# Loading the query weights of a decode kernel in two halves of 64 partitions, from two DMA queues

## The chip, the cores and the metric

The kernel runs on one core of one Trainium2 chip. The metric is device time in microseconds (us) for one execution, from the median of several runs. The core has a matrix engine (TensorE, PE in the profile), a vector engine (VectorE, DVE), a scalar engine (ScalarE, ACT), GpSimd (POOL) and SyncE (SP), which in this kernel only issues transfers. Sixteen DMA engines move data between main memory and the on-chip memory of 128 partitions. SyncE and ScalarE each issue DMAs through a queue of their own; in the profile SPq and ACTq are these issues, q1 is SyncE's queue and q10 is ScalarE's.

## What is computed

One token of decoding through attention with cached keys and values, and beside it a gated feed-forward layer; a scalar gate mixes both. All data are float32.

```python
def reference(A_x, A_k_cache, A_v_cache, A_wq, A_wo, B_x, B_w1, B_w3, B_w2, gate_w):
    x = A_x                                          # (1, 1, 512)
    g = sigmoid((x * gate_w).sum(-1, keepdims=True))
    q = (x @ A_wq) as 32 heads of 128                # A_wq (512, 4096)
    k, v = caches (8 heads, 32768, 128), each head used by 4 query heads
    p = softmax(q k^T * 128 ** -0.5)
    a = (p v) as one row of 4096 @ A_wo              # A_wo (4096, 512)
    b = (silu(x @ B_w1) * (x @ B_w3)) @ B_w2         # 512 -> 1792 -> 512
    return g * a + (1 - g) * b
```

The two caches are 134.2 MB each, and everything else together is some 28 MB. wq is 8.39 MB.

## The kernel before

The code does not leave its order to a scheduler. `Program.add` (L44) takes each operation with the names of what it reads and writes, works out the semaphore waits from them, and appends it to its engine's list. Each engine then runs its list in the order in which it was written.

Loads are full tiles of 128 partitions x 64 KB, 8.39 MB. Two such buffers exist, `big[0]` (big_a in the profile) and `big[1]` (big_b). `load` (L190) issues a DMA on SyncE. SyncE's list holds the loads in the order in which the data are used: wq into big_a, the first key tile into big_b, the second key tile into big_a, the third into big_b, then the weights of the feed-forward layer, then key tiles (big_a) and value tiles (big_b) in turn, and at the end the last values, wo and w2. A load waits until the readers of its buffer are through; SyncE then waits with it, and what is behind it in the list waits too.

The start goes as follows:

- ScalarE issues the rows of the token (x) and of the gate (gate_w), 2 KB each, into one partition of `probs` (L201 and L202). Both count on the semaphore `row`.
- SyncE issues wq into big_a (L203, through L194), keys "A0" and "A1", then the first key tile.
- GpSimd and VectorE build constants (L213 to L238).
- TensorE turns the token's row into columns by four small transposes (`columns`, L251), which wait for both rows; VectorE copies them into `xp` (L259).
- TensorE multiplies xp with wq, which has its 512 rows as 128 partitions x 4 chunks (`part`, L263, matmuls at L268). They wait for wq and for xp.
- One more product and an activation make the gate (L279, L280).
- ScalarE copies the products out (L286), VectorE transposes them into the two `kt` buffers (L289), and ScalarE copies them from there into `win` (L296), 16 small copies; `winc` (L324) is the part that TensorE uses as weights for scores.

Then 16 key tiles follow. VectorE transposes a tile in eight parts into the two `kt` buffers (L346; one of them shows as aside in the profile), ScalarE copies three quarters of its second half aside (L318), TensorE multiplies (L330), and the scores are copied out (L358). From the fifth tile on, value tiles are multiplied in the same loop (L432). The second key tile goes to the buffer in which wq was, so that its load waits for the matmuls at L268. The third waits until the first is worked off.

The semaphores of SyncE's loads are nine, used in turn (`load1` and so on); wq has `load1`.

Of the kernel before, what the change touches and what calls it, by code (L numbers as in the profile page):

```python
# [13 lines left out]
P = 128  # L14
# [102 lines left out]
def kernel(  # L117
# [13 lines left out]
    nc = tc.nc  # L131
# [5 lines left out]
    NC = D // P  # L137
# [17 lines left out]
    pr = Program(nc, tc.alloc_semaphore)  # L155
    pe, dve, act, pool = (
        lambda fn, _e=e, **kw: pr.add(_e, fn, **kw) for e in ("PE", "DVE", "ACT", "POOL")
    )
    V, A, T = nc.vector, nc.scalar, nc.tensor

    def sbuf(name, *shape):
        return nc.alloc_sbuf_tensor(name, [P, *shape], F32)[:]

    big = [sbuf("big_a", 2 * R), sbuf("big_b", 2 * R)]
# [25 lines left out]
    def load(dst, src, writes, over=()):  # L190
        lanes[0] += 1
        lane = f"load{lanes[0] % 9}"
        return pr.add(
            "SP", lambda: nc.sync.dma_start(dst, src), writes=writes, over=[*over, lane], inc=lane, by=16, also=lane,  # L194
        )

    def region(b, z):
        return big[b][:, z * R:(z + 1) * R]


    for i, t in enumerate((x.rearrange("a b n -> (a b) n"), gate_w.rearrange("(o n) -> o n", o=1))):  # L201
        pr.add("ACT", lambda i=i, t=t: nc.scalar.dma_start(rows[i][0:1, :], t), writes=[f"row{i}"], inc="row", by=16)  # L202
    load(big[0], wq.rearrange("(p c) n -> p (c n)", c=NC), ["A0", "A1"])  # L203


    ident, ones, fold = sbuf("ident", P), sbuf("ones", P), sbuf("fold", 32)
# [1 line left out]
    spot, mask, xp = sbuf("spot", 16, 8), sbuf("mask", 16), sbuf("xp", NC, 32)  # L208
# [16 lines left out]
    for src, dst, view, axes in (  # L225
# [11 lines left out]
            reads=[src], writes=[dst])  # L237
# [24 lines left out]
    for c in range(NC):  # L262
        def part(c=c):  # L263
            t = region(0, c // 2)
            for b in range(2):
                for j in range(4):
                    o = ((c % 2) * HKV + 4 * b + j) * REP * DH
                    ins = T.matmul(  # L268
                        pf[b][32 * j:32 * j + 32, :], xp[:, c, :], t[:, o:o + REP * DH],
                        start=(c == 0), stop=(c == NC - 1),  # L270
                    )
            return ins
        pe(part, reads=["A0", "A1", "xp"], writes=["f0", "f1"])


    gpr, gsm = tmp[0:1, 1].rearrange("p b d -> p (b d)"), sbuf("gsm", 1)
# [5 lines left out]
        reads=["gate0"], writes=["gate1"])  # L282
# [414 lines left out]
    a, b, c, d = flips  # L697
# [67 lines left out]
```

## Time and profile before

| | before |
|---|---|
| median of 3 runs | 694.1 us (693.98 to 695.0) |
| the profiled execution's own time | 693.89 us |
| its span, first to last instruction | 692.1 us |
| busy: PE, DVE, ACT | 388.3, 370.1, 134.7 us |
| bytes moved | 296.35 MB |
| transfers issued by SyncE, by ScalarE | 296.23 MB, 0.01 MB |

The profile shows one execution. A row of the timeline has the start, the time taken, the engine, the line of the program, the operation with its output and input, and in brackets how long the engine was idle before it and what ended that. A row of the windows has the stretch, the busy time of each engine in it, the granted clock of TensorE, the share of the 16 DMA engines that was busy, and the rate in GB/s. A short window counts a request where it begins, so that the share of one window can lie above 1 and that of the next at 0.

### The profile page before, as it was taken

How to read it: one execution, taken by the hardware profiler on the slowest of the kernel's cores; microseconds unless marked ns; L12 is line 12 of the kernel's file. 1: busy time of each engine (PE TensorE's matmuls, PEld its weight loads, DVE VectorE, ACT ScalarE, POOL GpSimd, SP SyncE). 2: the span in 40 equal slices, each digit the busy share in tenths (PEclk: the TensorE clock that was granted, in tenths of full speed). 3: DMA queues.
4: the chain of work that ended last, by engine and by line, in shares of the span. 5: the costliest groups of instructions: out<-in, count | busy, mean ns of one | idle time of the engine just before them, and what ended most of it. 6: DMA issues, size and time to landing. Idle time of an engine off the chain costs nothing. (4 is left out here: it accounts for less than half of the span.)

```text
span 692.1 us, 5789 instructions
## 1 busy us (share of the span) xinstructions
PE 388.3 (56%) x2448; PEld 95.3 (14%) x2448; DVE 370.1 (53%) x259; ACT 134.7 (19%) x113; POOL 2.8 (0%) x15
## 2 busy tenths in 40 slices
PE   1537677566473636565564646364563646564457
PEld 0101111201010101201010101101010101211112
DVE  1049998493725637493826537492816547600701
ACT  0143323222303131220303131220303031100000
POOL 1000000000000000000000000000000000000000
PEclk9969999968686966778695779788697879865789
DMA  9999999999999999999999999999999999999996
GB/s 394 444 432 424 428 424 432 449 439 432 424 432 424 443 447 432 428 428 428 432 443 443 428 428 428 428 443 447 432 424 428 428 436 439 421 451 425 422 429 287
DMA packets 6213, 296.35 MB, mean 428 GB/s; under 512 B 694, under 2 KB 698, under 8 KB 1084
## 3 DMA queue, kind: packets, MB, share of 16 engines
q1 hardware_dynamic: 6196, 296.23, 99.1%
q8 instruction: 6, 0.10, 0.1%
q14 instruction: 3, 0.02, 0.0%
q10 hardware_dynamic: 8, 0.01, 0.0%
HBM read 296.23 MB, written 0.00 MB: 428 GB/s over the span
## 5 line engine op out<-in xcount | busy, mean ns | idle before, releaser
L346 DVE STREAM_TRANSPOSE aside<-big_a 128x2048 f32<-128x2048 f32 x41 | 94.4, 2302 | 184.3 <-DMA big_a<-in_A_k_cache_dram 184.3
L330 PE MATMUL ps<-aside,winc 128*32 128x512 f32 x512 | 89.4, 776 | 168.0 <-PEq L703 167.2
L330 PE MATMUL ps<-kt,winc 128*32 128x512 f32 x512 | 89.0, 772 | 49.1 <-PEq L703 49.1
L318 ACT COPY aside<-big_a 128x6144 f32<-128x6144 f32 x14 | 74.4, 5313 | 171.2 <-DMA big_a<-in_A_k_cache_dram 171.2
L432 PE MATMUL ps<-big_b,pv 128*32 128x512 f32 x768 | 94.9, 650 | 17.4 <-PEq L703 17.4
L346 DVE STREAM_TRANSPOSE kt<-aside 128x2048 f32<-128x2048 f32 x32 | 72.7, 2273 | 0.0
L346 DVE STREAM_TRANSPOSE kt<-big_a 128x2048 f32<-128x2048 f32 x28 | 63.5, 2269 | 0.0
L330 PEld LDWEIGHTS ps<-aside,winc 128*32 128x32 f32 x512 | 13.1, 120 | 236.6 <-issue 236.6
L358 ACT COPY sb<-ps 128x512 f32<-128x512 f32 x16 | 17.1, 1071 | 136.5 <-PE ps L330 136.5
L432 PEld LDWEIGHTS ps<-big_b,pv 128*32 128x32 f32 x768 | 27.7, 119 | 85.0 <-issue 85.0
L346 DVE STREAM_TRANSPOSE aside<-aside 128x2048 f32<-128x2048 f32 x16 | 36.3, 2269 | 0.0
L587 PE MATMUL ps<-big_b,probs 128*32 128x512 f32 x128 | 19.1, 756 | 21.1 <-DMA big_b<-in_A_v_cache_dram 21.1
L330 PEld LDWEIGHTS ps<-kt,winc 128*32 128x32 f32 x512 | 13.1, 120 | 125.4 <-issue 125.4
L596 DVE TENSOR_SCALAR red<-ps,own_b 128x128 f32<-128x128 f32 x2 | 0.7, 350 | 52.7 <-PE ps L587 52.7
L324 ACT COPY winc<-win 128x128 f32<-128x128 f32 x32 | 9.8, 307 | 77.9 <-PE ps L330 77.9
L587 PE MATMUL ps<-big_a,probs 128*32 128x512 f32 x128 | 18.1, 730 | 7.6 <-DMA big_a<-in_A_v_cache_dram 7.6
L346 DVE STREAM_TRANSPOSE aside<-big_b 128x2048 f32<-128x2048 f32 x7 | 16.0, 2291 | 11.0 <-DMA big_b<-in_A_k_cache_dram 11.0
L641 PE MATMUL ps<-win,ones 128*128 128x512 f32 (+1 forms) x40 | 21.8, 631 | 0.0
L242 PE MATMUL ps<-acc 128*128 128x512 f32 x34 | 20.0, 670 | 2.5 <-POOL acc L213 1.5
L379 DVE TENSOR_REDUCE mt<-turned 128x8 f32<-128x2048 f32 x4 | 9.2, 2292 | 20.3 <-PE turned L368 20.3
L405 DVE TENSOR_REDUCE sums<-probs 128x8 f32<-128x2048 f32 x4 | 15.3, 3834 | 2.1 <-ACT probs L398 2.1
L268 PE MATMUL turned<-big_a,xp 128*32 128x512 f32 x64 | 8.6, 699 | 12.0 <-DMA big_a<-in_A_wq_dram 12.0
(94 smaller groups left out, 186.9 us busy)
## 6 DMA issues: line engine op xcount, KB each, us to landing
big_b<-in_A_v_cache_dram SPq DMA_DIRECT2D x2, 4096.0 KB, 25.8
big_b<-in_B_w_dram SPq DMA_DIRECT2D x2, 3584.0 KB, 20.8
aside<-in_A_wo_dram SPq DMA_DIRECT2D x1, 4096.0 KB, 29.4
big_a<-in_A_wo_dram SPq DMA_DIRECT2D x1, 4096.0 KB, 20.4
big_a<-in_B_w_dram SPq DMA_DIRECT2D x2, 1024.0 KB, 23.5
big_a<-in_B_w_dram SPq DMA_DIRECT2D x1, 768.0 KB, 26.0
big_a<-in_B_w_dram SPq DMA_DIRECT2D x1, 512.0 KB, 26.7
big_a<-in_B_w_dram SPq DMA_DIRECT2D x1, 256.0 KB, 26.9
```

The source lines that it names most:

```text
L242: return T.matmul(ps_s, acc[:, 0:P], acc, start=True, stop=False, skip_group_check=True)
L268: ins = T.matmul(pf[b][32 * j:32 * j + 32, :], xp[:, c, :], t[:, o:o + REP * DH], start=(c == 0), stop=(c == NC - 1),)
L318: act(lambda: A.copy(spare, src[:, :, 32:128]), reads=[key], writes=["wo"])
L324: lambda: A.copy(winc, win[:, t // 4, :, 16 - 16 * z:48 - 16 * z]),
L330: ins = T.matmul(ps_s[32 * g:32 * g + 32, :], winc[:, c, :], kt[c % 2][:, 512 * g:512 * g + 512], start=False, stop=False, skip_group_chec ...
L346: k = dve(lambda d=dst, s=src: V.transpose(d, s), reads=[key], writes=[f"kt{c % 2}"], credit="keys")
L358: lambda: A.copy(sb[:, :, :, t % 4], ps_s.rearrange("p (n i) -> p n i", i=32)),
L379: dve(lambda: V.tensor_reduce(mt[:, 0:8], turned.rearrange("p (n q) -> p q n", q=8), axis=AX.X, op=ALU.max), reads=banks, writes=["mt"])
L405: dve(lambda: V.tensor_reduce(sums[:, 8 * w:8 * w + 8].rearrange("p (u q) -> p u q", u=2), probs[:, :, 0:1024].rearrange("p u (n q) -> p u ...
L432: ins = T.matmul(ps_o[32 * t:32 * t + 32, :], pv[:, o:o + 32], big[1][:, n * P:(n + 4) * P], start=((z, g) == (0, 0)), stop=((z, g) == (1, ...
L587: ins = T.matmul(ps_o[32 * t:32 * t + 32, :], prob[u][:, o:o + 32], vt[:, n * P:(n + 4) * P], start=((e, z, g) == (0, 0, 0)), stop=((e, z, ...
L641: return T.matmul(bank[:, 0:n], ones, win.rearrange("p w c n -> p (w c n)")[:, 0:n], start=True, stop=True)
```

## The change

wq is cut in two halves of 64 partitions. SyncE loads partitions 0 to 63, ScalarE loads partitions 64 to 127. Both halves write to the places in big_a where wq was. ScalarE's half comes first in ScalarE's list, ahead of the rows of the token and the gate, which stay in their order. ScalarE's half has a semaphore `wq` of its own, and the matmuls wait for both.

```diff
+    wqd, half = wq.rearrange("(p c) n -> p (c n)", c=NC), P // 2
+    load(big[0][0:half], wqd[0:half], ["A0", "A1"])
+    pr.add("ACT", lambda: nc.scalar.dma_start(big[0][half:P], wqd[half:P]), writes=["wq"], inc="wq", by=16)
     for i, t in enumerate((x.rearrange("a b n -> (a b) n"), gate_w.rearrange("(o n) -> o n", o=1))):
         pr.add("ACT", lambda i=i, t=t: nc.scalar.dma_start(rows[i][0:1, :], t), writes=[f"row{i}"], inc="row", by=16)
-    load(big[0], wq.rearrange("(p c) n -> p (c n)", c=NC), ["A0", "A1"])
...
-        pe(part, reads=["A0", "A1", "xp"], writes=["f0", "f1"])
+        pe(part, reads=["A0", "A1", "wq", "xp"], writes=["f0", "f1"])
```

In the lists of the engines nothing else moves: ScalarE has one DMA more, ahead of the two rows; SyncE has as many as before, the first of them half as tall; TensorE's first product with wq waits for `load1`, `wq` and xp.

## The prediction, made before the changed kernel was run

> **What bounds the kernel now.** I read the page's transfer rows first, since a kernel that streams caches once can hardly be bound by anything else.
>
> ```profile
> span 692.1 us, 5789 instructions
> DMA  9999999999999999999999999999999999999996
> GB/s 394 444 432 424 428 424 432 449 439 432 424 432 424 443 447 432 428 428 428 432 443 443 428 428 428 428 443 447 432 424 428 428 436 439 421 451 425 422 429 287
> DMA packets 6213, 296.35 MB, mean 428 GB/s; under 512 B 694, under 2 KB 698, under 8 KB 1084
> q1 hardware_dynamic: 6196, 296.23, 99.1%
> q10 hardware_dynamic: 8, 0.01, 0.0%
> ```
>
> Every slice but the last is at 9 tenths or more, and SyncE's queue alone (q1) fills 99.1% of the 16 engines' time. The rate is the same for keys, values and weights. The span is 296.35 MB at this rate, plus a short start and tail. So a change here gains only if it fills a gap or raises the rate, and loses as much as it empties the transfer engines or slows them. ScalarE's queue (q10) carries nearly nothing today.
>
> Next I read the start, in the timeline and the list of waits.
>
> ```profile
> 0.93 0.40 SPq L194 DMA_DIRECT2D big_a<-in_A_wq_dram  x1
> 0.96 0.53 ACTq L202 DMA_DIRECT2D probs<-in_A_x_dram  x1
> 1.39 0.41 SPq L194 DMA_DIRECT2D big_b<-in_A_k_cache_dram  x1
> 1.52 0.23 ACTq L202 DMA_DIRECT2D probs<-in_gate_w_dram  x1
> 1.78 1.28 ACT L280 ACT_TABLE_LOAD   x1 [1.78 <-issue]
> 10.38 0.61 PE L253 MATMUL ps<-ident,probs 1*128 1x1 f32 x4 [6.76 <-DMA probs<-in_gate_w_dram]
> 11.02 0.17 DVE L259 COPY xp<-ps 128x4 f32<-128x4 f32 x1 [7.15 <-PE ps L253]
> 23.01 8.62 PE L268 MATMUL turned<-big_a,xp 128*32 128x512 f32 x64 [12.02 <-DMA big_a<-in_A_wq_dram]
> 31.69 0.33 SPq L194 DMA_DIRECT2D big_a<-in_A_k_cache_dram  x1
> 37.22 0.30 ACT L324 COPY winc<-win 128x128 f32<-128x128 f32 x1
> 43.30 2.31 DVE L346 STREAM_TRANSPOSE aside<-big_b 128x2048 f32<-128x2048 f32 x1 [9.34 <-DMA big_b<-in_A_k_cache_dram]
> 45.76 1.94 PE L330 MATMUL ps<-aside,winc 128*32 128x512 f32 x8 [13.82 <-PEq L703]
> 55.71 0.33 SPq L194 DMA_DIRECT2D big_b<-in_A_k_cache_dram  x1
> 62.65 2.31 DVE L346 STREAM_TRANSPOSE aside<-big_a 128x2048 f32<-128x2048 f32 x1 [1.62 <-DMA big_a<-in_A_k_cache_dram]
> ```
>
> wq lands just before 23.01, when the products of q start. xp has been ready since 11.19 (11.02 plus 0.17). SyncE issued the first key tile at 1.39, right behind wq, so the engines go on without a gap. The second key tile overwrites wq's buffer and is issued only at 31.69, when the products have read it; the first lands at 43.30. So that issue has 11.6 us to spare, less about 1 us from an issue to its first bytes (0.93 to the first busy window below). Then comes the third tile: issued at 55.71, 6.9 us ahead of the second one's landing at 62.65. Between 1 and 43 us the products, the copies and even the order of landing matter only as far as they delay one of these two issues past its spare time. What the engines themselves lose goes straight into the span.
>
> Last I cut the start into windows of one microsecond, to see how the engines move wq.
>
> ```profile
> 0.00:1.00 1.00, 0.00 (x0) 0.00 (x0) 0.00 (x0) 0.00 (x0) 0.24 (x5) 1.00 0.00 0
> 1.00:2.00 1.00, 0.46 (x1) 0.46 (x2) 0.00 (x0) 0.22 (x1) 0.77 (x3) 1.00 0.99 330
> 12.00:13.00 1.00, 0.00 (x0) 0.00 (x0) 0.48 (x1) 0.00 (x0) 0.00 (x0) 1.00 2.42 1049
> 13.00:14.00 1.00, 0.00 (x0) 0.00 (x0) 0.00 (x0) 0.00 (x0) 0.00 (x0) 1.00 0.00 0
> 17.00:18.00 1.00, 0.00 (x0) 0.00 (x0) 0.00 (x0) 0.00 (x0) 0.00 (x0) 1.00 2.42 1049
> 18.00:19.00 1.00, 0.00 (x0) 0.00 (x0) 0.00 (x0) 0.00 (x0) 0.00 (x0) 1.00 0.00 0
> ```
>
> The last two columns count a request where it starts. 1049 GB/s over 1 us is 1,048,576 bytes, or 16 requests of 64 KB, one row of wq for each engine. The share of 2.42 says that each takes 2.42 us. The window behind it is empty: the 16 engines start their requests within the same microsecond, round after round. wq is 128 rows, so 8 rounds, 19.4 us.
>
> **The change, part by part.** Removed is nothing: the same 8.39 MB go over the same engines.
>
> *The issue on ScalarE.* One DMA instruction is added ahead of the two rows and of the table load. At 0.40 to 0.53 us (the rows at 0.93 and 0.96) the table load moves from 1.78 to about 2.3. Its first user, the gate, runs after the products, so 28.9 us cover it. Cost 0. SyncE's half starts no sooner, since issues of a full tile already take only 0.40.
>
> *The new wait.* The products wait for both halves. Behind them on TensorE stand the gate's product and all scores; SyncE's second key tile waits for the products. The wait itself is a semaphore test, 0; what counts is when the halves land.
>
> *The halves.* No row here shows a load into 64 partitions, so I bound it. What all rows at 428 GB/s have in common is 16 engines and 128 partitions. A half keeps the engines and halves the partitions. If the engines set the rate, wq takes its 19.4 us as before: cost 0. If the receiving partitions set it, a round that goes to one half takes 4.84 us, and 8 rounds cost 8 x 2.42 = 19.4 us more. The two halves could make that good by running side by side, one engine of each pair on the lower half and one on the upper. Against that stand the windows: all 16 engines take their next request together, and with two queues served in turn they would all be on SyncE's half, then all on ScalarE's. The nearest row for service in turn is the gate's: 2 KB into one partition, issued at 1.52 beside SyncE's load, ended its wait at 10.38, 8.9 us or some 3.6 requests later. I take a value near the upper end. Engines that start apart by some tenths overlap less: with 0.12 us for the closest pair (an estimate; the spread is under 1 us by the windows), 8 x 0.12 = 1.0 comes off, which leaves 18.4. Bounds 0 and 19.4.
>
> [...]
>
> *The rows of the token and the gate.* They now stand behind ScalarE's half on its queue. Each is a data request and a landing, served one per request of SyncE's first key tile: between 0 (they land with wq) and 4 x 2.42 = 9.7 us behind wq. Then come the four transposes and the copy (10.38 to 11.19, 0.8 us) and the products (23.01 to 31.69 for the next issue, 8.7 us). Counted from wq's landing, the second key tile is issued at most 19.2 us later, its first bytes 1 us after that, where the first key tile needs 20.3 (43.30 less 23.01). So its spare time shrinks from 10.6 to about 0: cost 0, up to 2 if the landings spread as much as one request. On ScalarE the 16 copies into win end 5.8 us ahead of the first key tile now (37.52 to 43.30). They would end some 5 us behind it, so the first scores start up to 3 us later than their 45.76 after the landing. The third tile's 6.9 us cover that; without the cover each microsecond beyond would be one microsecond of empty engines. A delay of the first products costs nothing otherwise: nothing else waits for them.
>
> *Sum.* The profiled execution took 693.9 us for its span of 692.1, and the median of the runs is 0.2 above that. 693.9 + 18.4 + 0 = 712.3; against the median 712.5.
>
> **The rivals.**
>
> *The engines keep their rate (not slower).* Place: wq's 8 rounds. If the 64 KB in 2.42 us are an engine's own limit, or the engines fall out of step so that both halves are written at once, the halves together land at 23 us. For it speaks that nothing in the trace tells an engine's limit from a partition's; against it the joint start of the rounds. It decides from a pairing in which the partners are a full 2.42 us apart. The late rows then stay just inside the spare time: 694 to 696, most likely 694.1.
> [...]
>
> *Half the engines for each half.* If a half goes only to the eight engines that fill those partitions in a full tile, no partition is short. But SyncE's first key tile then starts at once on the eight engines that ScalarE's half needs, and the two alternate there: ScalarE's half takes 16 turns, 38.8 us instead of 19.4, and wq lands near 42.4. The rows land early. Products 42.4 to 51.0, second key tile issued at 51.1, bytes at 52.1, while the engines run dry about 1 us ahead of 43.30: 9.8 us empty, 703.7. For it: each engine has its own rows in a full tile, if the dealing goes by partition. Against: a full tile cannot show how fewer rows are dealt.
>
> *In between.* Some pairs out of step, or the lock lost after a few rounds: 3 to 15 us, 697 to 709.
>
> *Faster.* An earlier start is worth at most the 0.40 us of an issue, and the first slice at the best slice's 451 instead of 428 GB/s some 1 us on 8.39 MB. The two together reach 692.5.
>
> That the halves don't run at the same time is no case: the issues at 0.93 and 0.96 leave the same release.
>
> **How the numbers follow.** Lockstep on half the partitions 0.58 (709 to 716, at 712.5); eight engines each 0.13 (703.7); in between 0.09; engines keep their rate 0.17; faster 0.03. The range 700 to 717 takes in the first two and most of the third, 0.8 in all; its upper end is 693.9 + 19.4 + 2 and the 0.2 of the median, rounded up. The lower bound of the halves' cost, 0, is the fourth case and the part left out. A measurement of this kernel can tell about 0.2%, 1.4 us, from no change: slower by more than that 0.82 (the first three and the upper part of the fourth), within it 0.15, faster 0.03.
>
> **What would show it right or wrong.** In the changed kernel's page the first two or three slices would fall to half of 428 GB/s and the later ones stay where they are; DVE's first transpose of keys would move from 43.30 to about 61.7, and everything behind it by the same amount; q10 would carry 4.2 MB. The products would wait last for the gate's row, not for wq, and start some 8 to 10 us after wq's landing. If instead the slices stay at 394 and 444 and the first transpose at 43.3, the partitions were no limit. If the slices stay high and a gap stands near 43 to 52 us, it was the half engines. A loss that appears after 100 us would contradict all of these.

## The result and the profile after

The changed kernel takes 717.77 us (median of 4 runs, 716.95 to 718.25), the kernel before 694.04 us in the same comparison. The ratio is 1.0339 with a 95% interval of 1.0323 to 1.0354: 23.7 us slower. The forecast was 712.5 us, with 700 to 717 as its range. The direction and the mechanism were right; the size was not, and the time lies just above the range.

The page of the changed kernel, its span and its transfer rows (slices of 17.9 us):

```profile
span 715.2 us, 5790 instructions
DMA  9898999999999999999999999999999999999997
GB/s 235 176 352 353 466 414 422 457 412 451 429 429 447 414 451 429 422 451 418 444 433 425 447 422 444 429 418 458 418 444 433 418 458 418 421 453 422 424 429 292
q1 hardware_dynamic: 6132, 292.03, 96.0%
q10 hardware_dynamic: 88, 4.20, 2.8%
```

The first two slices move 235 and 176 GB/s where the kernel before moved 394 and 444, and yet the engines count as busy in them (9 and 8 tenths). That is the mark of a slow transfer, not of a missing one. The third slice holds the end of wq, the fourth (53.6 to 71.5 us) a real gap, as the windows will show. From the fifth on the rates are those of before: what is lost is lost by 72 us. q10 now carries the 4.2 MB of ScalarE's half.

The timeline of the changed kernel, in the rows that answer to those of before:

```profile
0.92 0.56 SPq L194 DMA_DIRECT2D big_a<-in_A_wq_dram  x1
0.96 0.56 ACTq L203 DMA_DIRECT2D big_a<-in_A_wq_dram  x1
1.55 0.57 SPq L194 DMA_DIRECT2D big_b<-in_A_k_cache_dram  x1
52.76 0.61 PE L255 MATMUL ps<-ident,probs 1*128 1x1 f32 x4 [49.15 <-DMA probs<-in_gate_w_dram]
53.40 0.17 DVE L261 COPY xp<-ps 128x4 f32<-128x4 f32 x1 [49.54 <-PE ps L255]
53.62 9.31 PE L270 MATMUL turned<-big_a,xp 128*32 128x512 f32 x64 [0.26 <-DVE xp L261]
63.00 0.33 SPq L194 DMA_DIRECT2D big_a<-in_A_k_cache_dram  x1
66.70 2.31 DVE L348 STREAM_TRANSPOSE aside<-big_b 128x2048 f32<-128x2048 f32 x1 [1.44 <-ACT win L298]
79.93 0.33 SPq L194 DMA_DIRECT2D big_b<-in_A_k_cache_dram  x1
```

The gate's row, not wq, ends the last wait ahead of the products: TensorE starts the transposes at 52.76 instead of 10.38, and the products at 53.62 instead of 23.01. The second key tile is issued at 63.00 instead of 31.69. The first transpose of keys starts at 66.70 instead of 43.30, and now it is ScalarE's copies into win that hold it up, no longer the key tile.

Windows of one microsecond, with the share of the 16 engines and the rate in the last two columns, counted where a request starts:

```profile
7.00:8.00 1.00, 0.00 (x0) 0.00 (x0) 0.00 (x0) 0.00 (x0) 0.00 (x0) 1.00 4.67 983
8.00:9.00 1.00, 0.00 (x0) 0.00 (x0) 0.00 (x0) 0.00 (x0) 0.00 (x0) 1.00 0.00 0
12.00:13.00 1.00, 0.00 (x0) 0.00 (x0) 0.00 (x0) 0.00 (x0) 0.00 (x0) 1.00 4.64 983
13.00:14.00 1.00, 0.00 (x0) 0.00 (x0) 0.00 (x0) 0.00 (x0) 0.00 (x0) 1.00 0.00 0
61.00:62.00 1.00, 1.00 (x16) 0.34 (x12) 0.00 (x0) 0.00 (x0) 0.00 (x0) 1.00 0.10 16
62.00:63.00 1.00, 1.00 (x14) 0.16 (x6) 0.00 (x0) 0.00 (x0) 0.00 (x0) 1.00 0.00 0
63.00:64.00 1.00, 0.24 (x2) 0.15 (x2) 0.20 (x2) 0.72 (x3) 0.00 (x0) 1.00 0.73 262
```

983 GB/s in 1 us are 15 requests of 64 KB. A share of 4.64 for 15 of 16 engines makes 4.95 us for each, where it was 2.42. The 16 still start together, now 5 us apart. From 61 to almost 64 us hardly any request starts: the first key tile is through, and the second one's issue at 63.00 brings its first bytes at about 64.

The trace keeps each request of the DMA engines, without the engine's number; chained by where one ends and the next begins, they fall into sixteen sequences. These are the durations, in us and in order, of one sequence of each kernel (S from SyncE's queue, A from ScalarE's; the kernels below the second row belong to the experiments). The first eight are wq, and what follows belongs to the first key tile:

```
before             S3.01 S2.42 S2.42 S2.42 S2.42 S2.42 S2.42 S2.42 | S2.42 S2.42 ...
the change         S5.00 A4.98 S4.95 A4.95 S4.95 A4.95 S4.95 A4.95 | S2.83 S2.42 ...
both on SyncE      S5.13 S5.12 S5.13 S5.13 S4.88 S5.12 S5.13 S5.13 | S2.84 S2.42 ...
rows first         S4.93 S5.12 A4.95 S4.94 A4.94 S4.94 A4.95 A5.11 | S3.12 S2.52 ...
32 partitions      S4.93 S5.13 S5.11 S5.12 S4.97 S5.12 S5.11 S5.12 | S2.84 S2.42 ...
16 partitions      S8.49 S9.36 S9.38 S9.38 S9.38 S9.38 S9.38 S9.38 | S3.69 S2.42 ...
even and odd       S3.21 S2.42 S2.42 S2.42 S2.42 S2.42 S2.42 S2.42 | S2.42 S2.42 ...
the same, 2 queues S3.16 A2.42 S2.42 A2.42 S2.42 A2.42 S2.42 A2.42 | S2.42 S2.42 ...
```

In the change the two queues are served strictly in turn, and the other engines have the same pattern at the same time, so all 16 write to the lower half together and then to the upper half together. That is read from the queues, of which each carries one half; the trace does not name the partitions of a request.

### The profile page after: what moved, and what is told of

Its sections match the earlier page's. It is cut to its first block, busy times and chain, and to the rows that moved or that the text cites. A ratio compares the mean times of both kernels' runs of the same rounds, so it can differ in the third digit from the quotient of the medians.

```text
span 715.2 us, 5790 instructions
## 1 busy us (share of the span) xinstructions
PE 386.5 (54%) x2448; PEld 96.4 (13%) x2448; DVE 370.2 (52%) x259; ACT 134.6 (19%) x113; POOL 2.8 (0%) x15
## 5 line engine op out<-in xcount | busy, mean ns | idle before, releaser
L332 PE MATMUL ps<-kt,winc 128*32 128x512 f32 x512 | 87.0, 756 | 48.5 <-PEq L705 48.5
L434 PE MATMUL ps<-big_b,pv 128*32 128x512 f32 x768 | 92.2, 635 | 17.5 <-PEq L705 17.5
L589 PE MATMUL ps<-big_a,probs 128*32 128x512 f32 x128 | 19.4, 776 | 8.2 <-DMA big_a<-in_A_v_cache_dram 8.2
## 6 DMA issues: line engine op xcount, KB each, us to landing
aside<-in_A_wo_dram SPq DMA_DIRECT2D x1, 4096.0 KB, 29.3
big_a<-in_A_wo_dram SPq DMA_DIRECT2D x1, 4096.0 KB, 19.4
```

The lines of the kernel that those rows point to most:

```text
L332: ins = T.matmul(ps_s[32 * g:32 * g + 32, :], winc[:, c, :], kt[c % 2][:, 512 * g:512 * g + 512], start=False, stop=False, skip_group_chec ...
L434: ins = T.matmul(ps_o[32 * t:32 * t + 32, :], pv[:, o:o + 32], big[1][:, n * P:(n + 4) * P], start=((z, g) == (0, 0)), stop=((z, g) == (1, ...
L589: ins = T.matmul(ps_o[32 * t:32 * t + 32, :], prob[u][:, o:o + 32], vt[:, n * P:(n + 4) * P], start=((e, z, g) == (0, 0, 0)), stop=((e, z, ...
```

## The experiments

The theory: two losses, one after the other. While wq is loaded, all 16 engines write to the same half of the partitions at a time, and a request takes 4.95 us instead of 2.42; and the rows behind ScalarE's half make the products, and with them the second key tile, late. Why such a request takes longer is not in the trace, which has durations and no paths. Rivals: two queues served in turn cost something of their own; the number of partitions, or of DMAs, decides; later loads catch up with the gap.

One more rival was not tried by a run of its own: half of the partitions is also one stretch of 4.19 MB of main memory, and the side that is read could be the slow one. The kernel before speaks against it. It loads wo in two such stretches of 4.19 MB, each into 128 partitions (L530), and the first of them, alone on the engines from 600 to 610 us, runs at the full rate, 433 GB/s, with 1.21 to 1.23 us for a request of 32 KB:

```profile
600.00:610.00 10.00, 6.41 (x28) 4.07 (x32) 4.37 (x10) 0.00 (x0) 0.00 (x0) 0.50 1.01 433
```

**Rows first.** The halves as in the change, the rows ahead of ScalarE's half.

```diff
+    for i, t in enumerate((x.rearrange("a b n -> (a b) n"), gate_w.rearrange("(o n) -> o n", o=1))):
+        pr.add("ACT", lambda i=i, t=t: nc.scalar.dma_start(rows[i][0:1, :], t), writes=[f"row{i}"], inc="row", by=16)
     load(big[0][0:half], wqd[0:half], ["A0", "A1"])
     pr.add("ACT", lambda: nc.scalar.dma_start(big[0][half:P], wqd[half:P]), writes=["wq"], inc="wq", by=16)
-    for i, t in enumerate((x.rearrange("a b n -> (a b) n"), gate_w.rearrange("(o n) -> o n", o=1))):
-        pr.add("ACT", lambda i=i, t=t: nc.scalar.dma_start(rows[i][0:1, :], t), writes=[f"row{i}"], inc="row", by=16)
```

> The changed kernel with the two rows issued ahead of ScalarE's half. Theory (two terms: the engines share too few partitions while they load wq, 19.1 us by the last engine's landing of the first key tile; and the late rows make the second key tile late, some 4 us): only the first term is left, 713 us, and no stretch without transfers near 62 us. Rival (the whole loss comes with the halves, the gap is only a consequence of the slower load): it stays at 717 to 718.

Measured: 715.59 us, ratio 1.0311 (1.0294 to 1.0328), between the two expectations. The gap is gone, but the order brought a cost of its own. ScalarE's half is issued only at 1.80 us, SyncE's queue gets two requests in before it, and a request that follows one of its own queue takes 5.1 us, one that follows the other queue's 4.95 (the list above). One engine, which had carried the gate's row, falls a turn behind: it is on its last request of wq until 47.4 us, for 4.84 us, when the fifteen others are on the first key tile. Fourteen of these take 2.9 to 3.4 us for their first request of that tile, one takes 4.82, about as long as the late engine's. The run shows that most of the loss has nothing to do with late rows; it does not size the two terms.

**Both halves from SyncE.** The rows alone are left to ScalarE.

```diff
...
-pr.add("ACT", lambda: nc.scalar.dma_start(big[0][half:P], wqd[half:P]), writes=["wq"], inc="wq", by=16)
+load(big[0][half:P], wqd[half:P], ["wq"])
```

> Both halves of 64 partitions on SyncE's queue, one behind the other; only the rows are on ScalarE's. Theory (partitions): each round of requests goes to one half of the partitions, so wq takes twice as long whoever issues it: 713 us, as with the rows first. Rival (two queues served in turn hinder each other): with one queue for wq nothing is lost, 694 us.

Measured: 715.47 us, ratio 1.0307 (1.0290 to 1.0325), 21.3 us above the kernel before. One queue loses as much as two. The queues are not the cause of this term; the theory's 713 was too low because requests take 5.12 us here.

**Halves by columns.** Two queues and rows behind ScalarE's half, as in the change, but each half has all 128 partitions.

```diff
-load(big[0][0:half], wqd[0:half], ["A0", "A1"])
-pr.add("ACT", lambda: nc.scalar.dma_start(big[0][half:P], wqd[half:P]), writes=["wq"], inc="wq", by=16)
+hc = NC * HQ * DH // 2
+load(big[0][:, 0:hc], wqd[:, 0:hc], ["A0", "A1"])
+pr.add("ACT", lambda: nc.scalar.dma_start(big[0][:, hc:2 * hc], wqd[:, hc:2 * hc]), writes=["wq"], inc="wq", by=16)
```

> The changed kernel with wq cut by columns: each half has 128 partitions of 32 KB, one from SyncE and one from ScalarE, the rows behind ScalarE's half as in the change. Theory: all 128 partitions are served in each round, wq lands at about 23 us as before; only the late rows are left: the second key tile is issued at about 42.5 us, its bytes start at 43.5 where the engines run dry between 41.2 and 42.8, which costs 1 to 3 us: 695 to 697. Rival (two queues): wq is slow here too, 713 to 718.

Measured: 697.41 us, ratio 1.0049 (1.0032 to 1.0066): 3.2 us, just above the theory's figure. Its timeline shows the second term alone:

```profile
32.43 0.61 PE L256 MATMUL ps<-ident,probs 1*128 1x1 f32 x4 [28.82 <-DMA probs<-in_gate_w_dram]
33.30 9.32 PE L271 MATMUL turned<-big_a,xp 128*32 128x512 f32 x64 [0.26 <-DVE xp L262]
42.70 0.33 SPq L194 DMA_DIRECT2D big_a<-in_A_k_cache_dram  x1
46.39 2.31 DVE L349 STREAM_TRANSPOSE aside<-big_b 128x2048 f32<-128x2048 f32 x1 [1.43 <-ACT win L299]
```

and its windows the gap that follows:

```profile
41.00:43.00 2.00, 1.93 (x18) 0.53 (x10) 0.00 (x0) 0.03 (x1) 0.00 (x0) 1.00 0.03 8
43.00:45.00 2.00, 0.00 (x0) 0.00 (x0) 1.46 (x3) 1.67 (x6) 0.00 (x0) 0.93 1.60 524
```

The rows end their wait at 32.43, 9.4 us behind the 23.01 at which wq had landed in the kernel before; the second key tile is issued at 42.70, and from 41 to 43 us the engines start next to nothing.

**Sixteen partitions at a time.** Eight loads from SyncE, rows first, against the kernel before:

```diff
-load(big[0], wq.rearrange("(p c) n -> p (c n)", c=NC), ["A0", "A1"])
+for i in range(0, P, 16):
+    load(big[0][i:i + 16], wqd[i:i + 16], ["A0", "A1"] if i == 0 else [f"wq{i}"])
...
-pe(part, reads=["A0", "A1", "xp"], writes=["f0", "f1"])
+pe(part, reads=["A0", "A1", *(f"wq{i}" for i in range(16, P, 16)), "xp"], writes=["f0", "f1"])
```

> wq in eight loads of 16 partitions from SyncE, one behind the other, the rows first on ScalarE's queue. [...] By partition: an eighth of the rate, 8 x 2.42 us each, 136 us more, 830. By the mere number of DMAs (some fixed cost of each): the six further DMAs beside two halves change little, 713 to 720.

Measured: 749.56 us, ratio 1.0802 (1.0784 to 1.0820), 55.3 us above the kernel before. A window shows what a request costs now:

```profile
20.00:21.00 1.00, 0.00 (x0) 0.00 (x0) 0.00 (x0) 0.00 (x0) 0.00 (x0) 1.00 5.88 655
```

655 GB/s are 10 requests; 5.88 x 16 / 10 is 9.4 us each. Eight times 9.38 less 2.42 makes 55.7. A request takes 3.9 times the 2.42 us of a full tile, and so the count of partitions (830, at eight times) and the count of DMAs (713 to 720) both fall; why it is 3.9 times is not shown.

**Waiting for the token's row alone.** The change with this edit only:

```diff
-        pr.add("ACT", lambda i=i, t=t: nc.scalar.dma_start(rows[i][0:1, :], t), writes=[f"row{i}"], inc="row", by=16)
+        pr.add("ACT", lambda i=i, t=t: nc.scalar.dma_start(rows[i][0:1, :], t), writes=[f"row{i}"], inc=f"row{i}", by=16)
-pe(columns, reads=["row0", "row1", "ident"], writes=["m0"])
+pe(columns, reads=["row0", "ident"], writes=["m0"])
```

> The changed kernel with one wait less: the transposes wait for the token's row alone, which lands two requests of the first key tile (4.9 us) ahead of the gate's; the gate's row is waited for only by the product that uses it. Halves and queues as in the change. Theory (the rows make the second key tile late): issued at about 58.1 us instead of 63.0, its bytes start at 59, ahead of the 60.4 at which the first engine runs dry; the stretch without transfers at 62 to 64 us is gone and with it 3.4 us: 714.4. Rival (the gap costs nothing, since later loads catch up): 717.8 as before.

Measured: 714.12 us, ratio 1.0295 (1.0278 to 1.0312), 3.65 us below the change. The timeline and the window at the place of the gap:

```profile
48.97 9.56 PE L270 MATMUL turned<-big_a,xp 128*32 128x512 f32 x64 [0.26 <-DVE xp L261]
58.60 0.33 SPq L194 DMA_DIRECT2D big_a<-in_A_k_cache_dram  x1
63.91 2.31 DVE L348 STREAM_TRANSPOSE aside<-big_b 128x2048 f32<-128x2048 f32 x1 [3.05 <-DMA big_b<-in_A_k_cache_dram]
```

```profile
60.00:62.00 2.00, 0.00 (x0) 0.00 (x0) 0.86 (x2) 1.54 (x9) 0.00 (x0) 0.71 1.08 459
```

The issue comes at 58.60 instead of 63.00, the window from 60 to 62 is full, and the first keys are waited for by VectorE again. This run splits the loss: 3.65 us for the late rows, 714.12 - 694.03 = 20.1 us for the halves. The split is good to about a microsecond, since the runs of the change spread from 716.95 to 718.25 us and these from 713.90 to 715.57. Nothing caught up with the gap later.

**Columns, rows first.** Against the halves by columns:

```diff
+    for i, t in enumerate((x.rearrange("a b n -> (a b) n"), gate_w.rearrange("(o n) -> o n", o=1))):
+        pr.add("ACT", lambda i=i, t=t: nc.scalar.dma_start(rows[i][0:1, :], t), writes=[f"row{i}"], inc="row", by=16)
     hc = NC * HQ * DH // 2
...
-    for i, t in enumerate((x.rearrange("a b n -> (a b) n"), gate_w.rearrange("(o n) -> o n", o=1))):
-        pr.add("ACT", lambda i=i, t=t: nc.scalar.dma_start(rows[i][0:1, :], t), writes=[f"row{i}"], inc="row", by=16)
```

> The halves by columns with the two rows issued first on ScalarE. Theory: nothing is left of either term, 694 us, though wq still comes from two queues. Rival (two queues cost something of their own): above 695.5.

Measured: 696.05 us (695.01 to 697.17), ratio 1.0034 (1.0020 to 1.0048). The theory's 694 was missed. The timeline points to the reason:

```profile
32.17 8.79 PE L271 MATMUL turned<-big_a,xp 128*32 128x512 f32 x64 [23.61 <-DMA big_a<-in_A_wq_dram]
41.02 0.33 SPq L194 DMA_DIRECT2D big_a<-in_A_k_cache_dram  x1
```

The rows were early, but ScalarE's half was now behind in time and stood in turn with the first key tile. On the engine that had carried the gate's row it was three turns behind, its last request ended at 29.3 us, and wq landed near 32 us instead of 23. The products were late once more, for another reason, and the second key tile was issued 9.3 us later than before. In the profiled run, the fastest at 695.01 us, most engines stand still for 0.4 to 1.5 us near 42 us for it, and their next requests take 2.6 to 3.25 us; that covers the 1 us which this run lost. The runs near 697 us left no trace. That two queues cost nothing by themselves, this run could not show; the last one does.

**Thirty-two partitions at a time.** As the eight loads, with four of 32.

```diff
-load(big[0], wq.rearrange("(p c) n -> p (c n)", c=NC), ["A0", "A1"])
+for i in range(0, P, 32):
+    load(big[0][i:i + 32], wqd[i:i + 32], ["A0", "A1"] if i == 0 else [f"wq{i}"])
...
```

> wq in four loads of 32 partitions (0 to 31, 32 to 63 and so on) from SyncE, rows first. [...] By partition count: a quarter of the rate, 58 us more: 752.

Measured: 715.41 us, ratio 1.0310 (1.0293 to 1.0327): the same as halves of 64 from SyncE, with 5.11 to 5.13 us for most requests there as here (the list above). The count of partitions (752) falls once more.

**Even and odd partitions from SyncE.** Still 64 partitions in each load, rows first.

```diff
-load(big[0][0:half], wqd[0:half], ["A0", "A1"])
-pr.add("ACT", lambda: nc.scalar.dma_start(big[0][half:P], wqd[half:P]), writes=["wq"], inc="wq", by=16)
...
+load(big[0][0:P:2], wqd[0:P:2], ["A0", "A1"])
+load(big[0][1:P:2], wqd[1:P:2], ["wq"])
```

> wq as two loads of 64 partitions from SyncE, the even ones and then the odd ones, rows first. By partition count: as the lower and upper half, 715.5. [...]

Measured: 694.61 us, ratio 1.0008 (0.9999 to 1.0018). Half the partitions in each load, and the full rate: but for the first one, its requests take 2.42 us.

**Even and odd from two queues,** else as the change:

```diff
-load(big[0][0:half], wqd[0:half], ["A0", "A1"])
+load(big[0][0:P:2], wqd[0:P:2], ["A0", "A1"])
-pr.add("ACT", lambda: nc.scalar.dma_start(big[0][half:P], wqd[half:P]), writes=["wq"], inc="wq", by=16)
+pr.add("ACT", lambda: nc.scalar.dma_start(big[0][1:P:2], wqd[1:P:2]), writes=["wq"], inc="wq", by=16)
```

> The change as it is, from two queues and with the rows behind ScalarE's half, but SyncE's half holds the even partitions and ScalarE's the odd ones. Theory (which partitions a half holds decides, not the queues): wq at the full rate, only the late rows are left, as with the halves by columns: 697 us. Rival (halves of 64 partitions from two queues cost something beside that): above 700.

Measured: 696.52 us, ratio 1.0038 (1.0024 to 1.0052). Only the choice of partitions differs from the change; the queues are served in turn as there, each request takes 2.42 us (the list above), and 21.3 of the 23.7 us are gone; the 2.5 us that are left are the late rows' cost, as the next run shows.

**The same, waiting for the token's row alone,** with the edit of the fifth run:

> The same, and the transposes wait for the token's row alone. Theory: both terms are gone, wq lands at about 23 us, the second key tile is issued near 38, ahead of the 41 at which the first engine runs dry: 694 to 694.6, as the kernel before. Rival (something of the change is left): above 695.5.

Measured: 694.41 us, ratio 1.0006 (0.9996 to 1.0015). With both terms taken out, the kernel from two queues takes as long as the one before, and not less: no version here beats it.

## Why the prediction was right in its mechanism and short in its size

The forecast of 712.5 us was 5.3 us short. Two terms of its sum were too small: the halves by 1.7 us and the rows by 3.65 us. Each measured above its own upper bound as well, so that the range, whose upper end was these bounds added up (715.5) and set a little higher (717), missed too.

*What bounds the kernel:* right. The loss sits in the first 72 us, every later slice has its old rate, and a gap of the engines went into the span.

*The issue on ScalarE and the new wait at 0:* right. The last run has both, and takes 694.41 us against 694.03 in the same comparison.

*The halves at 18.4 us, bounds 0 and 19.4:* the slower rounds came, the term was too small and even the upper bound was. It measured 20.1 us. Two steps failed. The 1.0 us taken off for engines that start apart, for which no row gave the 0.12 us, has no counterpart: all rounds after the first took their full time. And a request took 4.95 us instead of twice 2.42; 8 x (4.95 - 2.42) = 20.2. That the halves cost this and not the two queues is shown by both halves from SyncE, 715.47 us. That it matters which partitions a load holds, and not only how many, is shown by the others: with 32 in a row the kernel takes 715.41 us, as with 64 in a row, with 16 in a row 749.56, and with 64 even or odd ones 694.61. What makes the difference is not shown.

*The rows at 0, up to 2 us:* this step failed most. They measured 3.65 us in the change, and 2.5 to 3.2 us where wq itself kept its rate. The chain itself was nearly right: the second key tile was to be issued at most 19.2 us behind wq, and from the trace's last landing of a half, at 43.3 us, to the issue at 63.00 it was 19.7; the products took 9.31 us where 8.62 stood in the sum. Wrong was what it was held against. The spare time was counted to the landing of the whole first key tile, but an engine that is through with its own requests stands still from then on: in the changed kernel the engines are through at 61.5 to 61.9 us and hardly a request starts until 63.9. In the kernel before, that landing waited for one engine that ended its last request of the tile at 42.8 us, when the fifteen others had ended theirs by 42.0. The prediction itself has the engines run dry about 1 us ahead of 43.30 in one of its rivals, but not here. And engines that have run dry start slowly: fourteen of the sixteen take 2.7 to 3.15 us for their first request after the gap instead of 2.42; why is open. The sum of a gap of 2.1 to 3.6 us and a restart of half a microsecond was put at "about 0" because issue and landing seemed to meet; two numbers that meet are a risk, not a zero.

*The third tile's spare time as a cover:* right. It was issued at 79.93 and no further stretch without transfers follows.

*The rivals.* The engines keeping their rate, and half the engines for each half, are both ruled out by the rounds of 16 requests at 4.95 us. The faster start is ruled out by the last run, in which nothing is left to hide it.

## What to carry to other kernels

Before a load is cut, ask which partitions each piece holds, not how many queues issue it: requests to the lower or the upper half of the partitions took 4.95 us here, those to even or odd ones 2.42, and the halves by columns cost 3.2 us in all, late rows included. When a small row moves behind a large one, count its requests, one turn each (two for each row here, at 2.42 us a turn), and follow it to the next load that waits for its user. Measure spare time to the moment when the first engine has nothing to do, and allow for the restart, 2.7 to 3.15 us for the first request here.

## What the runs showed beyond expectation

The longer requests are no exact multiples. 64 KB took 2.42 us in full tiles and in even and odd halves, 27.1 GB/s for an engine. With 64 partitions in a row a request took 4.95 us when the requests came from two queues in turn, and 5.12 us in most rounds from one queue, 2.05 and 2.12 times as long. With 16 in a row it took 9.38 us, 3.88 times as long, less than four times. Why is open.

Every DMA of a row cost two turns on its engine, one for the 2 KB and one for the 4 bytes of its landing: the trace of the changed kernel has these at 44.72 and 47.23 us for the token's row and at 49.66 and 52.16 for the gate's, and two requests of the first key tile between the 2 KB of the one and of the other. With the wait for the token's row alone the products started at 48.97, with the wait for both at 53.62, 4.65 us or nearly two requests of 2.42 us later.

Who came first by less than a microsecond decided the order for tens of them here. With the rows first, ScalarE's half was issued at 1.80 us instead of 0.96, and wq landed by the start of the products at 50.68 us, where SyncE alone had it at 44.31.
